# Another queue for the first results, a later place for v of row 1 and an earlier one for a quarter of w_out

## The chip, the cores and the metric

The kernel runs on one core of one Trainium2 chip. The metric is the device time of one execution in microseconds. The span of a profile is the same execution from first to last instruction and is some 2 us shorter. Runs over 1.5% above the fastest of the same kernel are called slow and are left out of ratios.

## The reference, cut to what matters

Attention of 8 rows (batch entries), 8 heads, 576 tokens, head size 64; four heads look back over a window of 32 tokens, four over every fourth of 128. The result, 4608 tokens of 512 values, goes through two matrices with a squared ReLU between them.

```python
masks = np.stack([mask_plain if h < H // 2 else mask_dil for h in range(H)], axis=0)
scores = np.where(masks[None, :, :, :], scores, -1000000000.0)
...
attn = attn / (np.sum(attn, axis=-1, keepdims=True) + 1e-09)
return np.matmul(attn, v).astype(np.float32)
...
h = x @ w_in              # 512 -> 2048
r = np.maximum(h, 0.0)
return ((r * r) @ w_out).astype(np.float32)
```

## The kernel before

The tokens are cut into nine chunks of 512 for the matrices; attention goes row by row and its pieces are interleaved with the matmuls of the chunk before. In the profile, `ph` are the products with w_in, `po` those with w_out, `ps` and `pz` the scores, `pav` and `paw` the attention values, `px` and `py` their transposes, which ScalarE copies into `xT`. TensorE needs `xT` for `ph`.

GpSimd issues the loads that change the type (q, k, weights); SyncE issues v, the transposes and most stores. Each engine keeps its program order in these traces: ScalarE's `xT` copy at 69.93 us, whose `py` had been ready since 64.03, comes after a store that was issued only at 69.50. GpSimd also casts v (`vp`, `vd`) and reorders q and k of rows 2 and up (`nr`). A transfer is issued by an engine and lands later; a semaphore is a counter that it raises when it has landed, and an engine that needs the data waits for that count (the second transpose of row 2's reordered q and k landed at 66.92 us, and the GpSimd copy that waits for it began at 67.04).

```python
def store(c, t, po):
    ot = osb.tile([P, DM], FP32, name=f"ot{c}_{t}", tag="ot")      # three buffers
    nc.scalar.copy(ot, po)
    (nc.scalar if c == 0 else nc.sync).dma_start(out=out[...], in_=ot)

# the start: row 0, w_in, row 1, and the loads of row 2's q and k
cast_sliding_v(0)
load_w_in()                  # GpSimd's queue, three pieces: wi[0], wi[1], wi[2]
cast_dilated_v(0)
...                          # scores of row 0
load_w_out((0, 1))           # GpSimd's queue
nsd[1] = load_qk(1)          # GpSimd's queue
load_v(1)                    # SyncE's queue
cast_sliding_v(1)            # GpSimd, once v is there
load_w_out((2, 3))
cast_dilated_v(1)            # GpSimd, once v is there
ns = load_sliding_qk(2)      # GpSimd's queue
dd = keep_dilated_qk(2)
nr = by_token(2, ns)         # GpSimd
...                          # matrices of chunk 0, with row 1's attention between them
transpose_dilated(2, dd)     # SyncE's queue
transpose_sliding(2, keep_sliding_qk(2, nr))
load_v(2)
```

The softmax here doesn't subtract the row's maximum and nothing guards it: scores larger than these inputs give would overflow.

Of the kernel before, what the change touches and what calls it, by code (L numbers as in the profile page):

```python
# [13 lines left out]
P = 128  # L14
# [3 lines left out]
def kernel(  # L18
# [9 lines left out]
    nc = tc.nc  # L28
# [18 lines left out]
    NB = S // QB  # L47
# [25 lines left out]
    wi = [wpool.tile([P, NDM, w], FP16, name=f"wi{n}") for n, w in enumerate(wi_cols)]  # L73
# [9 lines left out]
    sv = stg.tile([P, NB, HH, D], FP32, name="sv")  # L83
    sd = stg.tile([P, 2, HH, DIL * D], FP32, name="sd")
# [5 lines left out]
    def load_qk(b):  # L90
        n = load_sliding_qk(b)
        m = natp.tile([P, 36 * D], FP16, name=f"nd{b}", tag="n")
        for i, s in ((1, k), (0, q)):
            nc.gpsimd.dma_start(
                out=m[64 * i : 64 * (i + 1), :],
                in_=s[b, HH:H].rearrange("h (p j) d -> (h p) (j d)", j=36),
            )
        return n, m

    def load_sliding_qk(b):  # L100
        n = natp.tile([P, HH, 9 * D], FP16, name=f"ns{b}", tag="n")
        for i, s in ((1, k), (0, q)):
            nc.gpsimd.dma_start(
                out=n[64 * i : 64 * (i + 1)],
                in_=s[b, 0:HH].rearrange("h (p j) d -> p h (j d)", j=9),
            )
        return n
# [8 lines left out]
    def load_sliding_v(b):  # L116
        for m in range(NB):
            lo = QB * m - PADP
            p0 = PADP if m == 0 else 0
            nc.sync.dma_start(  # L120
                out=sv[p0:P, m, :, :],
                in_=v[b, 0:HH, lo + p0 : lo + P, :].transpose([1, 0, 2]),
            )

    def load_dilated_v(b, eng):
        vv = v[b, HH:H].rearrange("h (i c) d -> i h (c d)", c=DIL)
        eng.dma_start(out=sd[PADD:P, 0, :, :], in_=vv[0:QD])
        eng.dma_start(out=sd[:, 1, :, :], in_=vv[QD - PADD : CL])

    def load_v(b):  # L130
        load_sliding_v(b)
        load_dilated_v(b, nc.sync)
# [9 lines left out]
    def load_w_out(gs):  # L142
        for g in gs:
            nc.gpsimd.dma_start(
                out=wo[g],
                in_=moe_w_out[4 * g * P : 4 * (g + 1) * P, :].rearrange(
                    "(fl s) m -> fl (s m)", s=4
                ),
            )
# [8 lines left out]
    def cast_sliding_v(b):  # L158
        for m in range(0, NB, 2):
            nc.gpsimd.tensor_copy(vp[b % 2][:, m : m + 2, :, 0:D], sv[:, m : m + 2, :, :])  # L160

    def cast_dilated_v(b):
        for t in range(2):
            for c in range(0, DIL, 2):
                nc.gpsimd.tensor_copy(  # L165
                    vd[b % 2][:, t, c : c + 2, :, 0:D],
                    sd[:, t, :, D * c : D * (c + 2)].rearrange("p h (c d) -> p c h d", d=D),
                )
# [52 lines left out]
    for m, w, pad in ((maskp, QB, PADP), (maskd, QD, PADD)):  # L221
        nc.vector.tensor_scalar(
            out=lo_[:, 0:w], in0=relf[:, 0:w], scalar1=-pad - 0.5, scalar2=None, op0=ALU.is_gt
        )
        nc.vector.tensor_scalar(
            out=hi_[:, 0:w], in0=relf[:, 0:w], scalar1=W - pad - 0.5, scalar2=None, op0=ALU.is_lt
# [7 lines left out]
    for r in range(2):  # L234
# [6 lines left out]
            out=vd[r][:, 0, :, :, D],  # L241
# [40 lines left out]
    def store(c, t, po):  # L282
        ot = osb.tile([P, DM], FP32, name=f"ot{c}_{t}", tag="ot")
        nc.scalar.copy(ot, po)  # L284
        (nc.scalar if c == 0 else nc.sync).dma_start(out=out[(c * 4 + t) * P : (c * 4 + t + 1) * P, :], in_=ot)

    def mm2_gen(c, g):
        for t in range(TOKC // P):
            po = pmool.tile([P, DM], FP32, name=f"po{c}_{t}", tag="pm")
            for ffc in range(NFF):  # L290
                mm2(c, g, po, t, ffc)
                if ffc % 2 == 1 and ffc < NFF - 1:
                    yield
            store(c, t, po)
            yield

    def mm2_by_rows_gen(c, g):

        pos = [
            pmool.tile([P, DM], FP32, name=f"po{c}_{t}", tag="pm") for t in range(TOKC // P)  # L300
        ]
        for f4 in range(0, NFF, 4):
            for t, po in enumerate(pos):
                for ffc in range(f4, f4 + 4):
                    mm2(c, g, po, t, ffc)
                    if ffc % 2 == 1 and ffc < NFF - 1:
                        yield
                if f4 + 4 == NFF:
                    store(c, t, po)
                    yield  # L310
# [223 lines left out]
        s_dilated(0, g)  # L534
    load_w_out((0, 1))
    nsd[1] = load_qk(1)
    load_v(1)
    cast_sliding_v(1)
    load_w_out((2, 3))
    cast_dilated_v(1)  # L540
    ns = load_sliding_qk(2)
    dd = keep_dilated_qk(2)
# [76 lines left out]
```

## Time and profile before

| | kernel before |
|---|---|
| time, median of 3 (at the prediction) | 335.85 us |
| span of the profile | 335.1 us |
| TensorE busy | 302.8 us, 90% |
| mean granted clock of TensorE (share of full speed) | 0.978 |
| longest wait of TensorE | 11.9 us, `ph` for `xT` |

The packed trace also holds the numbers of the semaphores, which `prof` doesn't print. In this profile the 136 transfers of SyncE and ScalarE raise eight of them in turn, 111 to 118, and GpSimd's 39 raise eight others, 99 to 106. ScalarE's first store waits for 112, which a sliding piece of row 2's v raises (landed at 69.43 us; the store is issued at 69.50), and then raises 112 itself; the second does the same with 115 and a dilated piece (landed at 77.79, issued at 77.86).

### The profile page before, as it was taken

The numbers are of one execution on the slowest core, as the hardware profiler recorded it, in microseconds if no ns is written. First come the engines' busy times: TensorE is split into PE (matmuls) and PEld (weight loads), VectorE is DVE, ScalarE is ACT, GpSimd is POOL, SyncE is SP. The second block draws the span as 40 slices with busy tenths as digits, with TensorE's granted clock in tenths as the row PEclk, the third lists the DMA queues.
The fourth block names the chain that finished last, engine by engine and source line by source line (L and its number), as shares of the span: only waits on it lengthen the run. The fifth ranks groups of instructions, "written<-read, shape, count | busy, mean of one in ns | idle before, by whom it ended". The sixth has DMA issues, their size and how long they took to land.

```text
span 335.1 us, 6199 instructions
## 1 busy us (share of the span) xinstructions
PE 302.8 (90%) x2452; PEld 158.9 (47%) x2452; DVE 163.3 (49%) x353; ACT 168.8 (50%) x286; POOL 75.0 (22%) x113
## 2 busy tenths in 40 slices
PE   1778888905999999999999999999999999999995
PEld 1553444402445554555555545545555555445542
DVE  6774347501965358625752595367436534302400
ACT  2735435213682577257626853684468436425711
POOL 4292512036500034303520361037000000000000
PEclk9999999975999999999999999999999999999999
DMA  7999999899801779478938991899291010011011
GB/s 130 224 195 237 215 209 128 197 218 241 171 2 63 154 183 220 113 174 177 228 94 198 203 232 64 183 201 223 82 184 46 33 64 31 2 63 63 3 61 64
DMA packets 79469, 46.67 MB, mean 139 GB/s; under 512 B 54352, under 2 KB 72784, under 8 KB 79440
## 3 DMA queue, kind: packets, MB, share of 16 engines
q1 hardware_dynamic: 64928, 31.60, 38.8%
q0 software_dynamic: 13936, 13.63, 25.3%
q10 hardware_dynamic: 576, 1.05, 0.9%
q8 instruction: 19, 0.31, 0.4%
q14 instruction: 10, 0.08, 0.1%
HBM read 39.85 MB, written 16.52 MB: 168 GB/s over the span
## 4 chain that ended last, share of the span: by engine, by line
PE 78%; DMA 10%; SPq 3%; DVE 3%; ACT 2%; POOL 1%; issue 1%; ACTq 0%; POOLq 0%
PE ph L259 36%; PE po L274 34%; DMA wi<-in_moe_w_in_dram 5%; DMA sd<-in_v_dram 3%; PE paw L445 2%; SPq L120 2%; PE ps L383 2%; DMA sv<-in_v_dram 2%; DVE AT L374 1%; PE pav L431 1%; PE pz L402 1%; DMA dp<-nr 1%; PE py L478 1%; PE px L460 1%; SPq L194 1%
## 5 line engine op out<-in xcount | busy, mean ns | idle before, releaser
L259 PE MATMUL ph<-xT,wi 128*128 128x512 f16 x576 | 132.4, 388 | 14.3 <-ACT xT L484 11.9
L274 PE MATMUL po<-wo,g 128*128 128x512 f16 x576 | 140.8, 379 | 0.0
L270 DVE TENSOR_TENSOR g<-rt 128x512 f16<-128x512 f16 x144 | 66.0, 461 | 112.6 <-ACT rt L269 112.0
L269 ACT ACTIVATE rt<-ph 128x512 f16<-128x512 f32 x144 | 85.9, 599 | 37.1 <-PE ph L259 35.4
L259 PEld LDWEIGHTS <-wi 128*128 128x128 f16 x576 | 64.6, 114 | 75.7 <-issue 17.4
L274 PEld LDWEIGHTS <-g 128*128 128x128 f16 x576 | 49.7, 97 | 46.3
L284 ACT COPY ot<-po 128x512 f32<-128x512 f32 x36 | 21.1, 586 | 53.1 <-PE po L274 51.9
L374 DVE TENSOR_TENSOR AT<-AT,maskd 128x576 f16<-128x576 f16 x32 | 24.1, 776 | 7.2 <-ACT AT L373 5.7
L466 ACT COPY xT<-px 128x576 f16<-128x576 f16 x16 | 10.2, 638 | 31.5 <-PE px L460 31.5
L417 DVE TENSOR_TENSOR x_d<-paw,rcp_d 72x512 f16<-72x512 f32 x32 | 22.0, 687 | 1.1
L484 ACT COPY xT<-py 128x576 f16<-128x576 f16 x16 | 10.2, 638 | 23.6 <-PE py L478 10.0
L204 POOL COPY seen<-QKTp 128x1 f16<-128x1 f16 x5 | 1.2, 240 | 93.1 <-DMA QKTp<-dp 93.1
L373 ACT ACTIVATE AT<-pz 128x576 f16<-128x576 f32 x32 | 19.0, 649 | 5.6 <-PE pz L402 5.4
L165 POOL CAST vd<-sd 128x512 f16<-128x512 f32 x32 | 19.2, 632 | 10.2 <-DMA sd<-in_v_dram 9.1
L160 POOL CAST vp<-sv 128x512 f16<-128x512 f32 x24 | 17.2, 746 | 15.1 <-DMA sv<-in_v_dram 14.9
L373 ACT ACTIVATE AT<-ps 128x576 f16<-128x576 f32 x32 | 19.0, 651 | 0.7 <-PE ps L383 0.5
L111 POOL COPY nr<-ns 128x2304 f16<-128x2304 f16 x6 | 12.8, 2125 | 29.3 <-DMA ns<-in_q_dram 19.6
L374 DVE TENSOR_TENSOR AT<-AT,maskp 128x576 f16<-128x576 f16 x32 | 14.9, 466 | 5.0 <-ACT AT L373 2.2
L417 DVE TENSOR_TENSOR x_p<-pav,rcp_p 96x512 f16<-96x512 f32 x24 | 16.5, 687 | 0.8
L445 PEld LDWEIGHTS <-AT 128*128 128x128 f16 x256 | 12.7, 102 | 8.8 <-PE paw L445 1.2
L416 DVE RECIPROCAL rcp_d<-paw 72x8 f32<-72x8 f32 x32 | 6.5, 203 | 19.5 <-PE paw L445 19.5
L445 PE MATMUL paw<-vd,AT 128*128 128x65 f16 x256 | 14.1, 199 | 1.1 <-POOL vd L165 0.7
(53 smaller groups left out, 132.7 us busy)
## 6 DMA issues: line engine op xcount, KB each, us to landing
out_dram<-ot SPq DMA_DIRECT2D x32, 256.0 KB, 2.0
sv<-in_v_dram SPq DMA_DIRECT2D x40, 128.0 KB, 5.0
sd<-in_v_dram SPq DMA_DIRECT2D x8, 512.0 KB, 11.6
dp<-nr SPq DMA_DIRECT2D x12, 288.0 KB, 3.5
ns<-in_k_dram POOLq DMA_DIRECT2D x8, 288.0 KB, 5.4
ns<-in_q_dram POOLq DMA_DIRECT2D x8, 288.0 KB, 7.0
sd<-in_v_dram SPq DMA_DIRECT2D x8, 288.0 KB
wo<-in_moe_w_out_dram POOLq DMA_DIRECT2D x4, 512.0 KB, 17.3
```

The costliest lines, as they stand in the source:

```text
L111: nc.gpsimd.tensor_copy(r.rearrange("x j h d -> x h j d"), n.rearrange("x h (j d) -> x h j d", d=D))
L160: nc.gpsimd.tensor_copy(vp[b % 2][:, m : m + 2, :, 0:D], sv[:, m : m + 2, :, :])
L165: nc.gpsimd.tensor_copy(vd[b % 2][:, t, c : c + 2, :, 0:D], sd[:, t, :, D * c : D * (c + 2)].rearrange("p h (c d) -> p c h d", d=D),)
L259: nc.tensor.matmul(ph, wi4[ffc // 4][:, dmk, :, ffc % 4], xs[:, dmk, :], start=(dmk == 0), stop=(dmk == NDM - 1),)
L269: nc.scalar.activation(rt, ph[:], ACTF.Relu)
L270: nc.vector.tensor_mul(g[:, ffc, :], rt, rt)
L274: nc.tensor.matmul(po, g[:, ffc, t * P : (t + 1) * P], wo[ffc // 4][:, ffc % 4, :], start=(ffc == 0), stop=(ffc == NFF - 1),)
L284: nc.scalar.copy(ot, po)
L373: nc.scalar.activation(AT[:, u, 0:UW], ps[:, :, 0 : UW // 2], ACTF.Exp, scale=scale)
L374: nc.vector.tensor_mul(AT[:, u, 0:UW], AT[:, u, 0:UW], mask)
L417: nc.vector.tensor_tensor(out=x[0:w], in0=pv[:, :, :, 0:D], in1=rcp[0:w].unsqueeze(3).to_broadcast([w, 2, HH, D]), op=ALU.mult,)
L445: nc.tensor.matmul(pav[:, e, h * (D + 2) : h * (D + 2) + D + 1], AT[:, 4 + h, off : off + P], vd[b % 2][:, t, 2 * a + e, h, 0 : D + 1], st ...
```

## The change

The intent: chunk 0's results no longer go through ScalarE's queue, whose stream also holds the copies that TensorE waits for. And v of row 1 is kept out of w_in's way: two tiny GpSimd copies write into `sv` and `sd` something read from the last piece of w_in, so that the loads that overwrite those tiles start only when it has landed. Of w_out, the third quarter now goes ahead of row 1's v, and only the last stays behind it.

```diff
-        (nc.scalar if c == 0 else nc.sync).dma_start(out=out[...], in_=ot)
+        (nc.gpsimd if c == 0 else nc.sync).dma_start(out=out[...], in_=ot)
 ...
     load_w_out((0, 1))
     nsd[1] = load_qk(1)
+    load_w_out((2,))
+    nc.gpsimd.tensor_copy(sv[64:P, :, :, 0], wi[2][64:P, :, 0:NB].rearrange("p d f -> p f d"))
+    nc.gpsimd.tensor_copy(sd[64:P, :, :, 0], wi[2][64:P, :, 0:2].rearrange("p d f -> p f d"))
     load_v(1)
     cast_sliding_v(1)
-    load_w_out((2, 3))
+    load_w_out((3,))
     cast_dilated_v(1)
```

More of the change, by code (lines that the diff above doesn't have):

```diff
@@ L284, in store @@
         nc.scalar.copy(ot, po)
-        (nc.scalar if c == 0 else nc.sync).dma_start(out=out[(c * 4 + t) * P : (c * 4 + t + 1) * P, :], in_=ot)
+        (nc.gpsimd if c == 0 else nc.sync).dma_start(out=out[(c * 4 + t) * P : (c * 4 + t + 1) * P, :], in_=ot)
     def mm2_gen(c, g):
```

## The prediction

> **What bounds the kernel now.** The page first: TensorE is busy 90% of the span and the other engines half of it or less, so the time is TensorE's work plus its holes and slow stretches. The slices (8.4 us each) say where those are.
>
> ```profile
> PE   1778888905999999999999999999999999999995
> PEclk9999999975999999999999999999999999999999
> DMA  7999999899801779478938991899291010011011
> ```
>
> From the 11th slice on, TensorE is full. Before it lie the start, a hole in the 9th and 10th slice (0, then 5), and a low clock in the same two (7, then 5). The transfer engines are full from 8 to 92 us, so whatever moves a transfer there pushes others. The view of waits names the holes:
>
> ```profile
> PE ph L259 <- ACT xT L484: 11.9, 1, 11.9
> PE ph L259 <- DMA wi<-in_moe_w_in_dram: 2.4, 1, 2.4
> ACT xT L484 <- DMA sd<-in_v_dram: 7.2, 1, 7.2
> ACT xT L484 <- DMA sv<-in_v_dram: 6.4, 1, 6.4
> ```
>
> The large one is a single wait for the copy of row 1's last attention values into xT, and that ScalarE copy waited twice for a load of v, which it doesn't read. The timeline around it:
>
> ```profile
> 66.43 0.59 PE L259 MATMUL ph<-xT,wi 128*128 128x512 f16 x2
> ...
> 69.50 0.38 ACTq L285 DMA_DIRECT2D out_dram<-ot  x1
> 69.93 0.64 ACT L484 COPY xT<-py 128x576 f16<-128x576 f16 x1 [6.45 <-DMA sv<-in_v_dram]
> 70.46 0.59 ACT L284 COPY ot<-po 128x512 f32<-128x512 f32 x1
> ...
> 77.86 0.34 ACTq L285 DMA_DIRECT2D out_dram<-ot  x1
> 78.24 0.64 ACT L484 COPY xT<-py 128x576 f16<-128x576 f16 x1 [7.19 <-DMA sd<-in_v_dram]
> 78.78 0.59 ACT L284 COPY ot<-po 128x512 f32<-128x512 f32 x1
> 78.93 12.85 PE L259 MATMUL ph<-xT,wi 128*128 128x512 f16 x46 [11.91 <-ACT xT L484]
> ```
>
> Read ScalarE's lines in order: results of chunk 0 are copied at 62.89, their store is issued only at 69.50, the first xT copy follows; the next store is issued only at 77.86, and the second xT copy, which TensorE wants, follows. ScalarE works in order, so each store that can't be issued holds the copies behind it. The stores wait for row 2's v: its first dilated piece, issued at 68.23 and 9.56 us long in the chain, lands at 77.79, 0.07 before the issue. No data connects them. [...]
>
> After the hole the clock is low:
>
> ```profile
> 67.10:78.90 11.80, 0.00 (x0) 0.00 (x0) 0.00 (x0) 1.79 (x4) 4.22 (x8) 0.66 1.07 233
> 78.90:82.00 3.10, 3.07 (x8) 1.12 (x8) 0.00 (x0) 1.40 (x3) 2.62 (x6) 0.50 0.89 208
> 82.00:84.00 2.00, 2.00 (x6) 0.61 (x5) 1.71 (x1) 1.34 (x3) 2.00 (x1) 0.50 0.92 247
> 84.00:86.00 2.00, 2.00 (x9) 0.97 (x8) 2.00 (x3) 0.83 (x2) 2.00 (x4) 0.86 1.08 306
> ```
>
> The columns are length, then busy us of TensorE, its weight loads, VectorE, ScalarE and GpSimd, then granted clock, DMA share and GB/s. The clock is 0.50 until some 84.5 us. The chain has 48 ph matmuls in 10.36 us at the full clock (113.78 us), 0.216 us each; the 46 after the hole took 12.85 instead of 9.93. The hole's second price is 2.9 us.
>
> The small hole is at the other end: the chain has the last piece of w_in issued at 18.22, 16.55 us under way, landing at 34.77, and TensorE idle from 32.40 to 34.82. All that time v of row 1 shares the transfer engines: its last piece was issued at 21.29 and took 16.7 us, to 38.0.
>
> [...]
>
> **Part 1, the store of chunk 0 through GpSimd.** It removes four issues from ScalarE (0.34 to 0.38 us each) and their waits: 6.45 and 7.19 us before the two xT copies. What ScalarE then does from 62.89: ot 0.58; xT as soon as py is in PSUM (about 64.05) 0.64; ot 0.59; xT 0.64. The second xT copy ends at about 66.0, before TensorE has done the two matmuls at 66.43 that don't need it. So the whole 11.9 us go, and without the hole the clock should stay full: 2.9 us more. Both lie on the path; TensorE is full from there to the end. GpSimd is idle from 55.7 to 67.0, waiting for the transposes of row 2, so four issues of some 0.65 us (its ns loads take 0.62 to 0.64) fit there. The semaphores of its queue that they take up were last used by transfers of before 51 us. New on it: the fourth ot copy needs the first store landed (three buffers). Issued at about 63.6 and landing in 2 to 4 us, it may hold ScalarE for some tenths; ph has four PSUM buffers, and the last is wanted only at about 69.
>
> **Part 2, v of row 1 behind w_in.** It adds two tiny GpSimd copies (estimate 0.3 us each) and moves 1.5 MB of v from 12 to 38 us to after w_in. How soon can w_in land alone? w_out pieces of 512 KB landed at 37.5 and 40.0 (21.19 + 16.3, 21.7 + 18.3), so 2.5 us per 512 KB; w_in is four such, 10 us[...]: 16.7 + 12 = 28.7, say 29. TensorE needs it at 32.4: the 2.4 us hole closes. TensorE then wants q and k of row 1 at 42.5 and 45.0 instead of 44.87 and 47.44; before they landed at 42.9 and 45.8. In GpSimd's queue they now start 5 us earlier, and share with v instead. By bytes I expect 42 to 45.8: up to 0.8 us of the 2.4 may be lost again.
>
> **Part 3, w_out.** Its last quarter is issued after row 1's sliding v is cast, some 38 to 46 us instead of 35.06. TensorE needs it at about 58 (it is the last third of the po pieces between 42 and 66 us), and in its queue it lands by some 51 anyway. No cost.
>
> **The sum.** 11.9 + 2.9 + 2.4 = 17.2 us; against it up to 0.8 for late q and k, some tenths for the fourth ot copy, and up to 0.5 because VectorE meets GpSimd's casts of rows 2 and 3 at another place: 1.3 in all. 335.85 - 17.2 + 1.3 = 319.9.
>
> **Rivals.** (a) Row 2 takes the place of the hole. Its q, k wait in GpSimd's order behind the casts of row 1's dilated v. If v[...] lands only at 48 to 50, they are issued at 52 instead of 39 to 43, the transposes end near 71.5 instead of 66.9, and v of row 2 follows 5 us later (casts to 85.5 instead of 80.7). TensorE wants the transposes at 75 (64 + 48 x 0.216), sliding v at 84 and dilated v at 88. That fits with some 3 us to spare; if it doesn't, 2 to 5 us come back: 322 to 325. For it: the transfer engines are full all along, and some of their time (17 to 19 us) is now unused. Against: the sum of bytes is the same, and before they had idled from 92 us on. (b) The large hole stays because ot, not the semaphore, is late: only the start would be gained, 333. Against: the copies of ot wait 1.3 us at most for TensorE, and the ACT lines name v. (c) The clock falls anyway, for being earlier in the program: 323. Against: it was 1.00 for the 65 us before the hole.
>
> **Range and chances.** The two large terms are one wait with a clear releaser and the slow clock that follows it; I trust them to within 1 us. The spread comes from (a) and from the end of the small hole. 317 to 325 should hold it eight times in ten. Faster by over 2% means under 329.1; that fails only if over 60% of the gain comes back: 0.95 for faster, 0.04 same, 0.01 slower.
>
> **What would show it.** Right: no releaser "ACT xT" for ph, ScalarE's xT copies near 64 and 65, the clock 1.00 from 60 to 100 us, w_in's last piece landed by 30, the first full stretch of ph at 10.4 us per 48. Wrong: TensorE idle between 42 and 50 with q or k of row 1 as releaser; idle at 75 or at 84 to 90 on QKTp or v of row 2; ScalarE idle before the fourth ot copy by over 1 us.

## The result, and the profile after

The changed kernel took 321.89 us (320.41 to 327.12, 4 runs) beside 335.67 for the kernel before. A ratio is the mean time of one kernel's fast runs over that of the other's of the same rounds, so it is not quite the ratio of these medians: 0.957, interval 0.949 to 0.965. In a later set of rounds it was 0.959 (0.953 to 0.964). The time predicted was 319.9 us, the range 317 to 325.

The slices of the span, now 8 us each, of the profile after:

```profile
PE   1679989999999799999999999999999999999995
PEclk9999999999999999999999999999999999999999
DMA  7999998999999894799379947894750110020011
```

The hole of the 9th and 10th slice and the low clock are gone. One 7 is new, in the 14th slice. The view of waits says what TensorE and ScalarE waited for:

```profile
ACT xT L484 <- PE py L478: 10.6, 15, 2.0
...
PE ps L383 <- DMA QKTp<-dp: 2.1, 1, 2.1
...
ACT ot L284 <- DMA out_dram<-ot: 1.4, 1, 1.4
```

No xT copy waits for v any more, only for the transposes it copies. ScalarE's timeline at the same place:

```profile
60.48 0.59 ACT L284 COPY ot<-po 128x512 f32<-128x512 f32 x1 [1.32 <-PE po L274]
61.66 0.64 ACT L484 COPY xT<-py 128x576 f16<-128x576 f16 x1 [0.59 <-PE py L478]
62.19 0.59 ACT L284 COPY ot<-po 128x512 f32<-128x512 f32 x1
62.67 0.66 ACT L484 COPY xT<-py 128x576 f16<-128x576 f16 x1
63.35 0.59 ACT L284 COPY ot<-po 128x512 f32<-128x512 f32 x1
65.35 0.59 ACT L284 COPY ot<-po 128x512 f32<-128x512 f32 x1 [1.40 <-DMA out_dram<-ot]
```

The six copies stand close together. Only the last waits, for the landing of the first store, whose buffer it takes. TensorE's timeline shows what follows: the whole stretch of ph in one piece, and later one new wait.

```profile
64.02 10.52 PE L259 MATMUL ph<-xT,wi 128*128 128x512 f16 x48
...
96.38 10.52 PE L259 MATMUL ph<-xT,wi 128*128 128x512 f16 x48
108.98 0.43 PE L383 MATMUL ps<-QKTp 64*128 64x96 f16 x12 [2.08 <-DMA QKTp<-dp]
```

The new wait is for the transposed q and k of row 3. The chain of waits of the profile after leads back from there in these steps; the left numbers are start and length:

```profile
64.29 6.19 DMA dp<-nr
...
75.69 9.66 DMA sd<-in_v_dram
87.17 11.85 DMA dd<-in_q_dram
99.04 1.30 SPq L198
100.43 3.47 DMA dp<-nr
103.92 1.28 SPq L194
105.30 3.65 DMA QKTp<-dp
```

Row 2's reordered q and k are written out late and slowly (6.19 us, beside the stores of chunk 0's results), row 2's v is loaded after them, row 3's q and k come behind the casts of that v, and their transposes end 2 us too late.

One profile of each kernel isn't enough here. The kernel before was looked at twice more and the changed kernel once more. Stages, in us, cut at TensorE's first `po` of chunk 0 and at the first `ph` of chunks 1, 2 and 3; the differences come from TensorE's timelines:

| stage | before | before, 2nd | before, 3rd | after | after, 2nd |
|---|---|---|---|---|---|
| start to chunk 0's `po` | 41.8 | 39.1 | 39.0 | 39.9 | 39.8 |
| to chunk 1's `ph` (row 1's attention) | 24.7 | 26.3 | 26.7 | 24.1 | 24.1 |
| to chunk 2's `ph` (the hole) | 47.2 | 44.9 | 46.2 | 32.4 | 34.2 |
| to chunk 3's `ph` | 32.5 | 32.4 | 32.4 | 34.5 | 33.1 |
| to the end | 188.9 | 188.7 | 188.5 | 189.1 | 188.8 |
| span | 335.1 | 331.3 | 332.8 | 320.0 | 320.0 |

The stages to chunk 2's and to chunk 3's `ph` take 32.4 us where TensorE waits for nothing. The hole's stage gave 10.7 to 14.8 us; the stage after it took 0.6 to 2.2 back.

### The profile page after: what moved, and what is told of

It is laid out like the page before. It is cut to its first block, busy times and chain, and to the rows that moved or that the text cites.

```text
span 320.0 us, 6200 instructions
## 1 busy us (share of the span) xinstructions
PE 300.9 (94%) x2452; PEld 158.9 (50%) x2452; DVE 155.3 (49%) x353; ACT 169.1 (53%) x286; POOL 77.3 (24%) x119
## 4 chain that ended last, share of the span: by engine, by line
PE 73%; DMA 12%; SPq 4%; DVE 3%; POOL 2%; ACT 2%; issue 1%; POOLq 0%; ACTq 0%
PE ph L259 32%; PE po L274 32%; DMA dd<-in_q_dram 4%; DMA dp<-nr 3%; DMA sd<-in_v_dram 3%; PE paw L445 2%; SPq L120 2%; DMA sv<-in_v_dram 2%; PE ps L383 1%; PE pz L402 1%; PE pav L431 1%; SPq L198 1%; DMA QKTp<-dp 1%; PE px L460 1%; PE py L478 1%
## 5 line engine op out<-in xcount | busy, mean ns | idle before, releaser
L259 PE MATMUL ph<-xT,wi 128*128 128x512 f16 x576 | 130.6, 385 | 0.0
L270 DVE TENSOR_TENSOR g<-rt 128x512 f16<-128x512 f16 x144 | 61.3, 426 | 101.6 <-ACT rt L269 101.0
L466 ACT COPY xT<-px 128x576 f16<-128x576 f16 x16 | 10.2, 639 | 30.2 <-PE px L460 30.2
L374 DVE TENSOR_TENSOR AT<-AT,maskd 128x576 f16<-128x576 f16 x32 | 19.3, 611 | 9.2 <-ACT AT L373 7.5
L160 POOL CAST vp<-sv 128x512 f16<-128x512 f32 x24 | 16.3, 701 | 29.7 <-DMA sv<-in_v_dram 29.7
L165 POOL CAST vd<-sd 128x512 f16<-128x512 f32 x32 | 19.3, 639 | 10.7 <-DMA sd<-in_v_dram 10.6
L374 DVE TENSOR_TENSOR AT<-AT,maskp 128x576 f16<-128x576 f16 x32 | 16.1, 511 | 6.2 <-ACT AT L373 3.9
```

The lines of the kernel that those rows point to most:

```text
L160: nc.gpsimd.tensor_copy(vp[b % 2][:, m : m + 2, :, 0:D], sv[:, m : m + 2, :, :])
L165: nc.gpsimd.tensor_copy(vd[b % 2][:, t, c : c + 2, :, 0:D], sd[:, t, :, D * c : D * (c + 2)].rearrange("p h (c d) -> p c h d", d=D),)
L259: nc.tensor.matmul(ph, wi4[ffc // 4][:, dmk, :, ffc % 4], xs[:, dmk, :], start=(dmk == 0), stop=(dmk == NDM - 1),)
L270: nc.vector.tensor_mul(g[:, ffc, :], rt, rt)
L374: nc.vector.tensor_mul(AT[:, u, 0:UW], AT[:, u, 0:UW], mask)
```

## The experiments

Twelve runs. The first four shared their runs of the kernel before, and so did the next four and the last four. A label names each.

**e1_stores_only: the first part alone.**

```diff
 # on the kernel before
-        (nc.scalar if c == 0 else nc.sync).dma_start(...)
+        (nc.gpsimd if c == 0 else nc.sync).dma_start(...)
```

> Only the first part: chunk 0's stores on GpSimd's queue, v of row 1 and w_out loaded as before. My theory (the stores on ScalarE cost 11.9 us of hole and 2.9 us of low clock; moving v gains 2.4 us at the start and loses 2.1 us at row 3): the 2.4 us wait for w_in at about 32 us is there again, the 11.9 us hole and the low clock are not, and the 2.1 us wait for QKTp at row 3 is gone. Span 335.1 - 14.8 = 320.3 us, within 0.5 us of the changed kernel. Rival (the row 3 wait comes from the stores, which sit in GpSimd's queue before the loads of row 3): the wait for QKTp stays, and the span is 322.4 us.

Measured: 323.78 us median, ratio 0.966 (0.958 to 0.973), span 321.7. The hole and the low clock are gone and there is no wait for QKTp at row 3, so the rival falls: the stores on GpSimd's queue don't cause that wait by themselves. Two things were not as expected. The wait for w_in was 0.27 us, not 2.4. And two waits were new, both of TensorE for VectorE, which was slow at the masks. VectorE in that run, in row 2's stage, and GpSimd beside it:

```profile
82.16 5.84 DVE L374 TENSOR_TENSOR AT<-AT,maskd 128x576 f16<-128x576 f16 x4
```

```profile
83.20 2.12 POOL L111 COPY nr<-ns 128x2304 f16<-128x2304 f16 x1
85.25 2.43 POOL L160 CAST vp<-sv 128x512 f16<-128x512 f32 x3
```

Four multiplies that elsewhere take 0.5 us each took 5.84 while GpSimd copied and cast. TensorE waited 2.22 us behind them there, and 1.74 us in row 1's stage behind the same meeting. There GpSimd's copy ran from 53.11 to 55.22, and the pair of multiplies begun at 53.49 took 2.40 us instead of 1.00; the first of the two ended 0.3 us after the copy, the second took 0.45. In row 2's stage the first multiply begins at 82.16, a full 1.0 us before the copy, and ends 0.3 us after it, at 85.65. No run here shows how the one holds up the other.

**e2_v_only: the other parts alone.**

```diff
 # on the changed kernel
-        (nc.gpsimd if c == 0 else nc.sync).dma_start(...)
+        (nc.scalar if c == 0 else nc.sync).dma_start(...)
```

> Only the other parts: v of row 1 behind w_in and three quarters of w_out ahead of it; chunk 0's stores on ScalarE as before. My theory: the start gains 2.4 us; the hole before ph of chunk 1 is there, and ends when the loads land whose semaphores the first two stores reuse, in this build the second dp store of row 2 and the first sliding v piece of row 2. In the changed kernel that piece lands near 75, so TensorE goes on at about 76 instead of 78.9, the low clock follows as before, and no wait is left at row 3. Span about 335.1 - 2.5 = 332.6 us. Rival (the large hole came from v of row 1 crowding the transfers, and moving v cures it): no hole at 64 us, span under 322 us.

Measured: 332.57 us median, ratio 0.992 (0.986 to 0.998), span 330.4. The rival falls: v was moved, and the hole stayed. ScalarE in this run:

```profile
67.58 0.38 ACTq L285 DMA_DIRECT2D out_dram<-ot  x1
68.00 0.64 ACT L484 COPY xT<-py 128x576 f16<-128x576 f16 x1 [7.46 <-DMA dp<-nr]
...
72.91 0.39 ACTq L285 DMA_DIRECT2D out_dram<-ot  x1
73.34 0.64 ACT L484 COPY xT<-py 128x576 f16<-128x576 f16 x1 [4.21 <-DMA sv<-in_v_dram]
```

This is the best evidence for the shared semaphores. The first store reuses the semaphore of the second `dp` store and the second store that of the first sliding piece of v; the stores waited for just these (7.46 and 4.21 us), named before the run, where the kernel before waited for two other transfers. By the numbers in the packed trace, ScalarE waits here for semaphore 114 before the first store and for 117 before the second, and these are the ones that those two transfers raise; in the first profile it waits for 112 and 115. `ph` went on at 74.03 us (76 expected) after a wait of 9.9, and its 46 matmuls took 12.39 us.

**e3_wout_whole: the last quarter of w_out in front of v too.**

```diff
 # on the changed kernel
-    load_w_out((2,))
+    load_w_out((2, 3))
 ...
-    load_w_out((3,))
```

> The changed kernel with the last quarter of w_out issued together with the third, ahead of row 1's v. Theory: w_out's last quarter is never waited for, so its place matters only by what it does to v. [...]v of row 1 lands 1 to 2.5 us later, row 2's q and k are issued that much later, and TensorE waits for QKTp at row 2 (it had 0.7 us to spare) and longer at row 3: span 320.0 + 1 to 3 us. Rival (place of the last quarter is free): span within 0.5 us of 320.0.

Measured: 324.77 us median, ratio 0.969 (0.963 to 0.975), span 323.2. TensorE waited for QKTp at both rows, 2.14 us at row 2 and 3.25 at row 3. So the place of the last quarter matters, though TensorE never waits for it: behind v it leaves v room. In this run row 1's sliding v was cast by 49.55 us, in the profile after by 47.57.

**e4_qk2_before_dilated_casts: row 2's q and k earlier.**

```diff
 # on the changed kernel
     load_w_out((3,))
-    cast_dilated_v(1)
     ns = load_sliding_qk(2)
     dd = keep_dilated_qk(2)
+    cast_dilated_v(1)
```

> The changed kernel with the loads of row 2's q and k issued by GpSimd before the casts of row 1's dilated v instead of after them. Theory (these loads wait in GpSimd's order behind the casts, which wait for v; that delay runs through the transposes and v of row 2 to the transposes of row 3): they are issued near 48 instead of 52 to 54, the transposes of row 2 end 3 to 4 us earlier, the 2.1 us wait for QKTp at row 3 goes, and the span is about 318 us. Rival (the row 3 wait comes from the transfer engines being full or from the stores on GpSimd's queue): the wait stays, and the span stays within 0.5 us of 320.0.

Measured: 321.25 us median, ratio 0.958 (0.953 to 0.964), span 318.4. The loads were issued at 47.56 to 49.46 us and no wait for QKTp is left in the waits of TensorE. The stage after the hole took 32.4 us. The rival falls. The gain in time, though, can't be told from scatter against the changed kernel's 0.957, which came from other rounds. Part of it was paid in row 1's stage: GpSimd's issues and the casts of dilated v now fall on VectorE's masks of row 1, whose first four multiplies took 4.37 us instead of 2.93, `pav` waited 1.05 us, and the stage took 24.8 us instead of 24.1 (24.9 in the repeat below).

**e0_after_again and e4_again: the changed kernel and that one, side by side.**

> The changed kernel once more, for a comparison on one chip and for the spread. Theory: a wait for QKTp at row 3 of some 1 to 3 us is there again, ScalarE copies xT without a wait for v, the clock stays at 1.00; span 319 to 321 us. If the wait at row 3 is absent and the span still near 320, it was an accident of one execution.

> The kernel with row 2's q and k issued before the casts of row 1's dilated v, beside the changed kernel in the same rounds. Theory: no wait for QKTp at row 3, about 1.5 to 2 us (0.5%) under the changed kernel. Rival (the earlier run's 318.4 against 320.0 was scatter): no difference, or the wait is there.

Measured: 323.06 us median for the changed kernel, ratio 0.959 (0.953 to 0.964), and 320.87, ratio 0.954 (0.949 to 0.959), for the other. Their intervals overlap: a gain is likely and not shown. In the changed kernel the wait for QKTp was there again, 1.14 us of it at row 2 this time and 0.3 at row 3, and `ph` waited 0.46 us for the fourth copy of results; in e4 it is absent for the second time. So the wait comes with this order of the loads, in both looks of it and in neither of e4; at which row it falls is scatter.

**e6_stores_only_late_casts: GpSimd held back while VectorE masks.**

```diff
 # on e1; seen is a one-column tile. Row 2's stage (b == 2) only
             load_v(b + 1)
-            nr = by_token(b + 1, ns)
-            cast_v(b + 1)
         pump(24)
         attn_scores(b, 4)
+        nc.gpsimd.tensor_copy(seen, AT[:, 7, 0:1])   # waits for the last mask
+        nr = by_token(b + 1, ns)
+        cast_v(b + 1)
```

> The kernel with only the stores moved to GpSimd's queue, and in the row 2 stage GpSimd's reordering of row 3's q and k and its casts of row 3's v held back until VectorE has masked the last scores of row 2. Theory (stores alone lost 2.3 us in that stage because VectorE's fp16 multiplies run slowly while GpSimd copies): the four maskd multiplies of row 2 take about 2 us instead of 5.84, the 2.22 us wait of pav for rcp_p goes, ph of chunk 1 to ph of chunk 2 is 32.4 us instead of 34.7. Rival (that loss has to do with the transfers or with ScalarE): the stage stays at 34 us or more.

Measured: 320.45 us median, ratio 0.955 (0.951 to 0.959), span 318.5. VectorE at the same masks, in two groups now:

```profile
81.56 1.23 DVE L374 TENSOR_TENSOR AT<-AT,maskd 128x576 f16<-128x576 f16 x2
83.06 1.00 DVE L374 TENSOR_TENSOR AT<-AT,maskd 128x576 f16<-128x576 f16 x2 [0.28 <-ACT AT L373]
```

2.23 us instead of 5.84, and the stage took 32.4 instead of 34.7. The rival falls. The kernel does without the move of v and is as fast as any here.

**e7_qk2_early_4_ot: a fourth buffer.**

```diff
 # on e4
-        ot = osb.tile([P, DM], FP32, name=f"ot{c}_{t}", tag="ot")
+        ot = osb.tile([P, DM], FP32, name=f"ot{c}_{t}", tag="ot", bufs=4)
```

> The kernel with row 2's q and k issued early, and four buffers instead of three for the copies of the results. Theory: the fourth copy no longer waits for the landing of the first store, so the 0.5 us wait of ph for ot at 67 us in the run before goes; up to 0.5 us under that kernel, span near 318. Rival: that wait is hidden; no difference.

Measured: 320.63 us median, ratio 0.955 (0.951 to 0.959), span 318.9. The wait of `ph` for ot is absent, but it was absent in e4_again too, with three buffers. No gain is shown.

**e5_stores_on_sync: the stores on SyncE's queue.**

```diff
 # on the kernel before
-        (nc.scalar if c == 0 else nc.sync).dma_start(...)
+        nc.sync.dma_start(...)
```

> The kernel before with chunk 0's stores on SyncE's queue. Theory (what counts is whose in-order stream the store's wait stands in): ScalarE is free, so the 11.9 us hole and the low clock go, as on GpSimd's queue; but now the transposes of row 2 stand behind the stores in SyncE's order, start near 67 instead of 55 and end near 79, after TensorE wants them (76): a wait for QKTp of about 2.5 us at row 2, again about as much at row 3, perhaps 1 us for v. Span about 326 us (323 to 329). Rival (any queue other than ScalarE's does the same): span 320 to 322.

Measured: 325.39 us median, ratio 0.972 (0.965 to 0.979), span 323.7. The hole went, the transposes of row 2 began at 66.58 us, and `ps` of row 2 waited 2.80 us for QKTp; both as expected. No wait for QKTp was left at row 3. In the wait's wake the clock fell to 0.55, and eight `ph` took 3.56 us instead of some 1.9. So a store costs what stands behind it in its engine's order: a hole of 9.7 to 11.9 us behind ScalarE's, a wait of 2.80 us behind SyncE's.

**e8_stores_only_all_late: GpSimd held back in row 1's stage as well.**

```diff
 # on e6
-    nr = by_token(2, ns)
     attn_values(0, 0)
 ...
     attn_scores(1, 2, 1)
+    nc.gpsimd.tensor_copy(seen, AT[:, 7, 0:1])
+    nr = by_token(2, ns)
```

> As the kernel with the stores alone and the late casts, and in row 1's stage too GpSimd's reordering of row 2's q and k held back until VectorE has masked row 1's last scores. Theory: the 1.7 us wait of pav for rcp_p in row 1's stage goes too, and nothing waits for the reordered q and k, which have some 8 us to spare; span about 316.8 us, faster than the changed kernel's 318 to 320, although v of row 1 is where it was. Rival: the wait moves to another place; span 318.5 as in that run.

Measured: 320.58 us median, ratio 0.959 (0.955 to 0.964), span 318.9. The wait for rcp_p in row 1's stage went, but `pd` waited 0.84 us for q of row 1 and the first masks met the casts of v instead. The rival was right: nothing gained.

**b1_before_look and b2_before_look: the kernel before, unchanged.**

> A second look at the kernel before. Theory: the hole before ph of chunk 1 is there with 11 to 12 us, behind ScalarE's stores that wait for v of row 2. Open: the wait of ph for w_in at the start was 2.4 us in the first profile, but only 0.3 us in the run with the stores alone, whose start is the same program. If it is scatter of the start, this look shows another value between 0 and 3 us.

> A third look at the kernel before, for the same: size of the large hole (11 to 12 us) and the scatter of the wait for w_in (0 to 3 us).

Measured: 333.10 and 334.53 us, spans 331.3 and 332.8 (one run each; their profiles are read for waits, not for time). The waits of TensorE in the second look:

```profile
PE ph L259 <- ACT xT L484: 9.7, 1, 9.7
...
PE pav L431 <- DVE rcp_p L416: 2.8, 2, 1.6
```

The third look has 11.2 and 2.9. Neither lists a wait of `ph` for w_in, of which the first profile had 2.4.

## Why the prediction was right or wrong

**The hole (11.9 us): right, and the larger term.** ScalarE's stores waited for unrelated transfers and held the xT copies. e1 takes the stores away and the hole goes; e2 keeps them, moves v and the hole stays, with the releasers that were named before the run (7.46 and 4.21 us); e5 takes another queue and the hole goes too. The size was one execution's: 9.7 and 11.2 us in the other two looks. Rival (b), a hole because ot is late, fell with it.

**The low clock (2.9 us): right.** In the second look the 46 matmuls after the hole took 12.76 us, 2.8 over 9.93. With the hole gone, 48 took 10.52 at a clock of 1.00, so rival (c) fell. Hole and clock account for the stage of the kernel before: 32.4 + 9.7 + 2.8 = 44.9, as the table has it. One reading of the prediction was wrong here without harm: the clock was not 1.00 for all of the 65 us before the hole. The clock records of the traces begin near 26.5 us, and up to there the view shows 9 for want of a record; the first `ph` matmuls take 634 ns there, as they do after the hole (631 ns), and 379 ns later.

**The 2.4 us at the start: mis-sized, and the step that failed.** The prediction put it as "TensorE needs it at 32.4: the 2.4 us hole closes". The last piece of w_in did land at 30.2, near the estimate of 29, whose allowance for the start no trace shows; the two small copies behind it took 0.22 and 0.46 us, and v's loads were issued from 30.50. But that hole was one execution's: in the other two looks of the kernel before, and in e1, whose start is the same program, ph waited 0.3 us or less. There w_in was issued at 14.8 to 15.5 us against 16.70, because row 0's v happened to land earlier. Chunk 0's `po` began at 41.8 us in the first profile alone, and at 38.9 to 40.0 in the thirteen others, of every kernel here. Against the looks the changed kernel gains nothing before it (39.9 against 39.1). The 0.9 us lost fit the slow first matmuls, of which the profile after had 12 and the second look 7. Five more at some 0.21 us each (0.427 us from start to start instead of 0.216) are an estimated 1.1 us:

```profile
L259 PE MATMUL ph<-xT,wi x12: 524/634/634, 23.6 to 28.3; 128*128 128x512 f16 x12
L259 PE MATMUL ph<-xT,wi x7: 577/634/634, 23.5 to 26.1; 128*128 128x512 f16 x7
```

These are the profile after and the second look, until the clock rises at 28.63 and 26.48. The changed kernel gains in the next stage, 24.1 us against 26.3 and 26.7 (24.7 in the first profile), where the prediction expected up to 0.8 of loss. The four profiles with v moved and GpSimd's order otherwise kept (two of the changed kernel, e2, e3) all have 24.1, and e1, e5 and e6, without the move, 25.7 to 25.9. In the looks of the kernel before, GpSimd's reordering of row 2's q and k falls on the last masks of row 1, and `pav` waits up to 1.6 and 1.9 us; in the profile after it starts at 57.86, when they are done, and the longest such wait in the stage is 0.34. That this is the cause is supported, not settled: e8 holds the reordering back without moving v and its stage still took 25.2 us, with the 0.84 us wait for q of row 1 in it.

**Rival (a): it came, at or under the low end of its 2 to 5 us.** The times are those worked out: q and k of row 2 issued at 52.17 (52 predicted), the copy that waits for their transposes at 73.74 (71.5), the casts of row 2's v to 86.6 (85.5). TensorE wanted the transposes at 74.5 (the prediction's 64 + 48 x 0.216 is 74.4, not 75), so 0.7 us were to spare instead of 3, and the delay surfaced a row later as 2.08 us, in the second run as 1.14 at row 2. e4 moves these loads forward and the wait goes. What was missed of it: the stores of chunk 0, now early, meet the write of `dp`, whose second piece took 6.2 us in both looks instead of the 3.7 to 4.0 of the kernel before. That they slow it fits e5, where the stores had landed first and it took 3.7, but no run isolates it.

**The fourth ot copy and w_out: right in kind.** ScalarE waited 1.40 us for the first store's landing, and TensorE 0 and 0.46 us behind it. The last quarter of w_out was never waited for; e3 shows that its place behind v is worth some 3 us of span, which "No cost" didn't see as a gain.

**VectorE meeting GpSimd (up to 0.5 us): too small in general.** The changed kernel was spared, e1 was not: 1.74 and 2.22 us. In the changed kernel the wait for QKTp costs about as much as one of these. That fits how little the move of v adds to the stores: 0.966 for e1 against 0.957 and 0.959, with intervals that overlap, and e6, which avoids the larger meeting, reaches 0.955 without the move.

The measured median lies 2 us above the 319.9 predicted. That is about what rival (a), left out of the sum, took (1.4 to 2.1 us), and also no more than the scatter of the fast runs (320.1 to 324.1 in both sets). The term at the start that wasn't there was largely made good by the gain in row 1's stage that the prediction had not counted. That the number came out so close is in this part luck. The sum also has a slip: 0.8, 0.5 and "some tenths" for the fourth ot copy are more than its 1.3.

## What to carry to other kernels

A transfer issued by a compute engine can wait for a semaphore whose earlier user is a slow load elsewhere, and everything behind it in that engine's order waits too (6.45 and 7.19 us on ScalarE, 11.9 us on TensorE in the first profile): issue stores from an engine with nothing urgent behind them. Take the size of a wait from several executions before counting it as a gain; a wait of one profile in the crowded start may be scatter (2.4 us for w_in in one look, 0.3 or less in the two others). A load moved back in one queue delays what stands behind its consumers (2.08 us for QKTp at row 3 in the profile after); follow that chain two stages on, and watch where the copies of GpSimd meet VectorE (four multiplies in 5.84 us beside them in e1, in 2.23 apart from them in e6).

## What the runs show of the clock, the stores and their semaphores

- The clock: in these runs it did not follow from the length of the wait alone. In the first profile it was 0.50 after the hole of 11.9 us and 1.00 after that of 2.4; a wait of 2.80 us was followed by 0.55 (e5), one of 3.25 us (e3) by 1.00. What decided it was not shown. After the large hole the low clock lasted 5.6, 5.4 and 3.8 us in the three looks at the kernel before, 4.7 in e2.
- The choice of the engine that issues a store counted by what stands behind the store in its order: the same four stores, all other code equal, gave spans of 331.3 to 335.1 us from ScalarE, 323.7 from SyncE and 321.7 from GpSimd.
- The semaphores: in the first profile and the profile after, the transfers of SyncE and ScalarE take eight in turn (111 to 118), and in the first profile two stores so held ScalarE for 6.45 and 7.19 us behind loads they have nothing to do with.
